# A Fourier layer with a soft mixture of experts on one core: expert weight loads moved away from the last batch's two DRAM round trips, and each round trip's loads put on two DMA queues

## The chip, the core and the metric

The kernel runs on one core of a Trainium2 chip. The engines named here are PE (TensorE, matrix products), DVE (VectorE), ACT (ScalarE), POOL (GpSimd) and SP (SyncE, which in this kernel only issues DMAs). The metric is device time in microseconds (us) of one execution, the median of several. Before the change it is 558.88 us (three runs, 558.2 to 559.1).

## The reference: what is computed

For each of 8 batches x is 2496 tokens by 256 channels, float32. A real Fourier transform runs along the tokens, then a complex linear layer over the channels, a soft threshold at 0.01 and the inverse transform. The result, 19968 tokens by 256, goes through a soft mixture of 8 experts with 4 slots each:

```
logits = x @ phi                                    # 19968 x 32
d = softmax of logits over the tokens (each slot over all 19968)
slot_input = d.T @ x                                # 32 x 256
h = max(slot_input[e] @ w1[e], 0); slot_out[e] = h @ w2[e]      # w1: 8 x 256 x 1024, w2: 8 x 1024 x 256
c = softmax of logits over the slots (each token over its 32)
out = c @ slot_out
```

The softmax over tokens joins all batches: the expert layers can start only when the last batch has been through the whole chain, and the output only when the expert layers are done.

## The kernel before, in words

The transform of length 2496 is split into 39 by 64. A main loop of 40 steps (8 batches with 5 groups of frequencies each) does the forward transform, the complex layer and the threshold. PE, DVE, ACT and POOL all work in it. Times in the code's tables count a step as 4 units, and TB is the time at which the last step's work is over.

Behind the loop each batch has a chain (c_stages, and last_chain for batch 7) that forms logits, their exponentials and the weighted sums of the slots without ever forming the inverse transform of all channels. In it the data changes its layout twice, and each time through DRAM: `g_sb` is written to `gd` and read back as `gp` with the axes exchanged (first trip), and `ea` is written to `ed` and read back as `eb` (second trip). The reads are in pieces of 32 numbers, 128 bytes. For batches 0 to 6 the chain runs inside the main loop; for batch 7 nothing is left to run beside it except the transposes `pt` of batches 6 and 7 (tp_t: PE transposes, ACT and DVE copy the result to the tiles `T`) and the sums `pr` of batch 6.

The chain of batch 7 on the engines is: `pg` (PE), `g_sb` (ACT), write `gd`, read `gp`, `pL` (PE), maximum and `L`, `pm`, `pb`, exponential `ee` (ACT), `pe` (PE), `ea`, write `ed`, read `eb`, `pd` (PE), `dd` (DVE), `pr`, `psl`. Then come the expert layers: first `hps` (all 16 tiles of w1), `hs`, `pht`, then `po` (all 16 tiles of w2); and then the output: `cin` (stored combine weights of batches 0 to 5, read back), `chl` (their split in two parts by ACT and DVE), `pc`, `so`, `prep`, and 78 products `pq` whose copies `ost` are written out.

The expert weights are 32 loads of 512 KB (16 MB), w1 first; load number i is called wi here, from w0 to w31. The table `PLAN["T_"]["wl"]` gives for each load its time against TB and the tile it goes to: 'r', 'a', 'x', 'T', 'h', 't' name pools of tiles that are free by then ('x' and 'T' are two half loads of 256 KB each). The pool behind 'h' (hl_tile, tag "hl") has 9 buffers (NHL, the third number of `PLAN["nw"]`), which the output tiles `ost` use later. A tile pool gives its buffers out in turn, and a load into a buffer that was used waits for the last reader of what was in it.

Every engine works in the order in which its instructions were recorded, so an instruction that waits holds up everything behind it on its engine. All DMAs are issued by SP on one queue. Each DMA takes the next of 8 semaphores in turn (DMAHW0 to DMAHW7), and waits at issue until the DMA eight places before it has landed.

## Time and profile before

| | before |
|---|---|
| time, median of 3 runs | 558.88 us (558.2 to 559.1) |
| time of the profiled execution | 556.67 us |
| its span, first to last instruction | 554.5 us |
| granted TensorE clock | 0.994 |
| PE busy | 520.4 us (94%) |
| DVE, ACT, POOL busy | 433.3, 299.7, 287.2 us |
| DMA traffic | 115.95 MB, mean 209 GB/s |
| chain that ended last | PE 64%, DVE 16%, DMA 9%, ACT 4%, issue 4% |

The profiled execution is 2.2 us faster than the median of the runs; its span is 2.17 us shorter than its own time. In a row of a timeline stand start and duration in us from the span's start, engine, line, operation, what is written and read, and in brackets how long the engine was idle before and what ended that. "SPq" rows are DMA issues on SP's queue; their duration is the issue, not the transfer. A row of the chain of waits has start, duration and what the program's end hung on then. A row of the windows has the stretch, its length, busy us and instruction counts of PE, PE's weight load, DVE, ACT and POOL, the granted clock, the mean busy share of the 16 DMA engines, and GB/s. Line 227 is the helper that issues a DMA from SP, line 174 the one that records the operations of DVE, ACT and POOL, line 233 the one for matrix products.

### The profile page before, as it was taken

What the parts mean: (1) busy time and instruction counts of PE and PEld (TensorE: products, weight loads), DVE (VectorE), ACT (ScalarE), POOL (GpSimd) and SP (SyncE); (2) the same over time, 40 slices, a digit from 0 to 9 for tenths busy, and PEclk for the clock granted to TensorE, in tenths of its full rate; (3) what the DMA queues carried; (4) which work ended last, traced back from release to release, by engine and by line L of the source; (5) the groups of instructions that cost most, each with busy time, mean ns of one, the idle gap of its engine ahead of it and who ended that gap; (6) DMA issues with size and microseconds to landing.
All of it is one profiled execution on the core that took longest, in us unless ns stands there. A gap on an engine that the chain in (4) does not pass through costs nothing.

```text
span 554.5 us, 11971 instructions
## 1 busy us (share of the span) xinstructions
PE 520.4 (94%) x4455; PEld 448.9 (81%) x4455; DVE 433.3 (78%) x853; ACT 299.7 (54%) x662; POOL 287.2 (52%) x262
## 2 busy tenths in 40 slices
...
GB/s 304 187 172 168 133 201 168 193 175 201 192 179 180 178 189 189 164 190 201 177 178 180 186 202 155 241 211 204 186 83 130 105 177 299 379 252 363 365 373 356
DMA packets 90181, 115.95 MB, mean 209 GB/s; under 512 B 46482, under 2 KB 65872, under 8 KB 90124
## 3 DMA queue, kind: packets, MB, share of 16 engines
...
q14 instruction: 22, 0.18, 0.1%
...
## 4 chain that ended last, share of the span: by engine, by line
PE 64%; DVE 16%; DMA 9%; ACT 4%; issue 4%; SPq 1%; POOL 1%; ACTq 0%; DVEq 0%; POOLq 0%
PE py L233 14%; PE px L233 9%; PE pq L233 8%; PE pa L233 7%; PE pk L233 6%; PE pt L595 4%; PE pr L233 3%; DMA eb<-ed 3%; PE pc L1083 2%; DVE mx L174 2%; DVE xtl L174 2%; DMA ed<-ea 2%; DVE ut L174 1%; DVE clpL L174 1%; PE pe L233 1%
## 5 line engine op out<-in xcount | busy, mean ns | idle before, releaser
L174 POOL TENSOR_TENSOR rt<-ut,rt 128x512 f32<-128x512 f32 x79 | 112.4, 1423 | 21.1 <-DVE rt L174 17.4
L174 POOL TENSOR_TENSOR xsl<-xsm,xsh 128x256 fp32r<-128x256 f32 x78 | 59.8, 766 | 108.1 <-DVE xsh L174 76.0
L174 POOL TENSOR_TENSOR xl<-xr,xh 117x512 fp32r<-117x512 f32 x74 | 100.9, 1364 | 16.4 <-ACT xh L174 8.6
L233 PE MATMUL px<-smov,ap 128*128 128x128 f32 x640 | 86.1, 278 | 2.5 <-DVE xsm L174 1.6
L233 PEld LDWEIGHTS px<-smov,ap 128*128 128x128 f32 x640 | 80.5, 193 | 8.7 <-PE pa L233 2.5
L174 ACT CAST xth<-px 128x512 fp32r<-128x512 f32 x80 | 46.9, 586 | 64.1 <-PE py L233 34.2
L174 DVE SCALAR_TENSOR_TENSOR ut<-py,pk,k 128x256 f32<-128x256 f32 x160 | 69.4, 474 | 12.9 <-PE py L233 11.0
L174 ACT COPY ast<-pa 128x512 f32<-128x512 f32 x77 | 45.3, 588 | 57.7 <-PE pa L233 57.6
L174 DVE TENSOR_TENSOR xtl<-px,xth 128x512 fp32r<-128x512 f32 x80 | 54.5, 682 | 20.8 <-ACT xsm L174 20.6
L233 PE MATMUL py<-xth,nwsh 128*128 128x256 f32 x160 | 53.4, 334 | 0.0
L174 DVE TENSOR_SCALAR rt<-ut 128x512 f32<-128x512 f32 x69 | 50.9, 738 | 0.5
L233 PE MATMUL pk<-xsh,w_rh 128*128 128x256 f32 x160 | 48.2, 301 | 0.0
L174 ACT COPY T<-pt 128x512 f32<-128x512 f32 x70 | 42.0, 601 | 9.0 <-PE pt L595 7.3
L595 PE MATMUL pt<-pk,rt 128*128 128x128 f32 x320 | 45.8, 273 | 0.9 <-DVE dd L174 0.6
L233 PE MATMUL pk<-xsl,w_rh 128*128 128x256 f32 x160 | 45.4, 284 | 0.3 <-POOL xsl L174 0.3
L233 PE MATMUL pk<-xsh,w_rl 128*128 128x256 f32 x160 | 45.1, 282 | 0.0
L233 PE MATMUL py<-xtl,wdh 128*128 128x256 f32 x160 | 44.7, 279 | 0.0
L233 PE MATMUL py<-xtl,nwsh 128*128 128x256 f32 x160 | 44.7, 279 | 0.0
L233 PE MATMUL py<-xth,wdl 128*128 128x256 f32 x160 | 44.7, 279 | 0.0
L233 PE MATMUL py<-xth,wdh 128*128 128x256 f32 x160 | 44.6, 279 | 0.0
L233 PE MATMUL py<-xth,nwsl 128*128 128x256 f32 x160 | 44.6, 279 | 0.0
L233 PE MATMUL pq<-rhs,ct 128*128 128x512 f32 x156 | 41.8, 406 | 0.3 <-DVE ost L174 0.3
...
## 6 DMA issues: line engine op xcount, KB each, us to landing
...
```

What stands on the lines that cost most here:

```text
L174: return lambda *a, **k: self.tc.keep_in_program_order(f(*a, **k))
L233: tc.keep_in_program_order(nc.tensor.matmul(**kw))
L595: tc.keep_in_program_order(nc.tensor.transpose(out=out, in_=in_, identity=identity))
L1083: nc.tensor.transpose(out=pc[:, i * P1 : (i + 1) * P1], in_=chls[b][x][:, 2 * (r + i) : 2 * (r + i) + 2].rearrange("p g h s -> p (g h s)") ...
```

## The change

Three things change.

Place and time of the weight loads. Four loads (w3 to w6) move to 42 units before TB, in the main loop, into the room of two tiles (`atr`) that only the head of the program needs; these tiles move from the main loop's pool to one of their own ("hd"). No load stands any more between the end of the main loop and the first trip, nor behind the read of the first trip. Four loads (w15 to w18, 'H') are issued by ACT, behind the copies of `L`. The last 13 stand behind the read of the second trip on SP: w19 and w20 as 'T', w21 and w22 as 'x', w23 to w28 as 'h', w29 to w31 as 't'.

Queues. `gp` is read by four DMAs, two on SP and two on ACT, and `eb` by two, one on SP and one on ACT. Both reads are recorded earlier in the program's order (the numbers behind TB).

Transposes. The first group of batch 7's transposes (pt_0) is recorded at TB + 0.9 and so stands ahead of `pL` rather than behind `pr` of batch 6.

```
--- before.py
+++ after.py
@@ -142,7 +142,7 @@
     "ko": 0.915,
     "to": 0.7,
     "late": {'6': {'cms': [19.75, 19.71, 860.75, 862, 864, 865], 'pd': [20.36, 20.37], 'pr': [31.55, 31.6, 31.65, 31.7, 31.75], 'pL': [5.4, 5.8], 'pm': 6.875, 'pb': 7.325, 'pe': [8.75, 9.75], 'pg': [0.875, 1.275], 'fr': {'sinv': 0, 'm2': 0, 'f1': 0, 'suni': 0}}, '5': {'pg': [1.1, 1.8], 'pL': [4.95, 5.75], 'pm': 6.8, 'pb': 7.15, 'pe': [9.2, 9.9], 'pd': [13.8, 14.8], 'pr': [15.0, 17.25, 19.5, 21.75, 24.0]}, '4': {'pr': [18.4, 20.49, 24.49, 28.49, 32.49]}},
-    "T_": {'wl': [[-45, 'r'], [-44, 'r'], [-43, 'r'], [-31.0, 't'], [-30.7, 't'], [-29.4, 't'], [-27.6, 't'], [-27.8, 't'], [-11, 'a'], [-10.3, 'a'], [-9.6, 'a'], [-7.5, 'x'], [-6.4, 'x'], [1.11, 'x'], [1.07, 'h'], [1.08, 'h'], [1.09, 'h'], [1.1, 'h'], [1.11, 'h'], [13.55, 'h'], [13.1, 'h'], [13.6, 'h'], [13.6, 'h'], [13.61, 't'], [13.61, 't'], [13.61, 't'], [13.61, 't'], [13.61, 't'], [13.7, 'T'], [13.7, 'T'], [13.7, 'T'], [13.7, 'T']], 'cl': 16, 'cp': 46.5, 'ct': 46.6, 'du': [[-4.5, 0], [-2.4, 0], [1.2, 0]], 'd1': [5, 2, 4, 0, 0, 0], 'cm': [19.9, 19.91, 19.92, 25, 25.1, 25.2], 'cm7': [18, 20, 22, 23, 25, 27], 'ye': 0.2, 'te': [[5.6, 0.2], [5.5, 0.4]], 'pg': [-7, -3.25, -0.35], 'yt': 0.5, 'wr': -30.6, 'tp': [0, 0.9, 1.05, 0.5], 'tt': [[-0.4, 0.5, 0.6, 0.7, 0.8], [12, 12.1, 12.2, 12.3, 12.4]], 'z': 13.55, 'th': [0.1, 0.12], 'tl': [0.2, 0.25]},
+    "T_": {'wl': [[-45, 'r'], [-44, 'r'], [-43, 'r'], [-42, 'e'], [-41.9, 'e'], [-41.8, 'e'], [-41.7, 'e'], [-31.0, 't'], [-30.7, 't'], [-29.4, 't'], [-27.8, 't'], [-27.6, 't'], [-11, 'a'], [-10.3, 'a'], [-9.6, 'a'], [10.3, 'H'], [10.31, 'H'], [10.32, 'H'], [10.33, 'H'], [13.56, 'T'], [13.57, 'T'], [13.58, 'x'], [13.59, 'x'], [13.6, 'h'], [13.6, 'h'], [13.6, 'h'], [13.6, 'h'], [13.6, 'h'], [13.6, 'h'], [13.61, 't'], [13.61, 't'], [13.61, 't']], 'cl': 16, 'cp': 46.5, 'ct': 46.6, 'du': [[-4.5, 0], [-2.4, 0], [1.2, 0]], 'd1': [5, 2, 4, 0, 0, 0], 'cm': [19.9, 19.91, 19.92, 25, 25.1, 25.2], 'cm7': [18, 20, 22, 23, 25, 27], 'ye': 0.2, 'te': [[5.6, 0.2], [5.5, 0.4]], 'pg': [-7, -3.25, -0.35], 'yt': 0.5, 'wr': -30.6, 'tp': [0, 0.9, 1.05, 0.5], 'tt': [[-0.4, 0.5, 0.6, 0.7, 0.8], [0.9, 12, 12.1, 12.2, 12.3]], 'z': 13.55, 'th': [0.1, 0.12], 'tl': [0.2, 0.25]},
     "f1": [1.5, 2.15],
     "ap1": 1.9,
     "f0": 0.2,
@@ -182,6 +182,7 @@
     pp = ctx.enter_context(tc.tile_pool(name="pp", bufs=2, space=bass.MemoryType.PSUM))
     dr = ctx.enter_context(tc.tile_pool(name="dr", bufs=2, space=bass.MemoryType.DRAM))
     wcp = ctx.enter_context(tc.tile_pool(name="wc", bufs=1, side="right"))
+    hdp = ctx.enter_context(tc.tile_pool(name="hd", bufs=1, side="left"))
     wm = tc.tile_pool(name="wm", bufs=1, side="left")
     wa = tc.tile_pool(name="wa", bufs=1, side="right")
     wmp, wap = wm.__enter__(), wa.__enter__()
@@ -349,6 +350,9 @@
 
     qps, at0, atr = {}, [], []
 
+    def hd_tile(h, name):
+        return hdp.tile([128, 2 * (K1 - KG) * NP], F32, tag=f"hd{h}", name=name)
+
     def q_mm(i, h):
         qd, k = divmod(i, 2)
         if k == 0:
@@ -409,7 +413,7 @@
         yield t_[0]
         for h in range(2):
             at0.append(wtile([128, G, S], F32, ("L", "ee")[h], f"at0_{h}").rearrange("p g s -> p (g s)")[:, : 2 * KG * NP])
-            atr.append(wmp.tile([128, 2 * (K1 - KG) * NP], F32, tag=f"at{h}", name=f"atr{h}"))
+            atr.append(hd_tile(h, f"atr{h}"))
         for i in range(6):
             for h in range(2):
                 q_mm(i, h)
@@ -842,7 +846,7 @@
     w1 = [(0, c, 2 * j + q) for q in range(2) for c in range(2) for j in range(4)]
     w2 = [(1, h, 2 * j + q) for h in range(2) for q in range(2) for j in range(4)]
     wlist = w1 + w2
-    wbuf = {}
+    wbuf, early = {}, []
 
     def at(t, fn, *a):
         def one():
@@ -870,7 +874,16 @@
             src = t["moe_w1"][e, h * 128 : h * 128 + 128, :]
         else:
             src = t["moe_w2"][e, h * 512 : h * 512 + 512, :].rearrange("(p f) d -> p (f d)", f=4)
-        if loc == "r":
+        q = aq if loc.isupper() and loc != "T" else sp
+        loc = loc if loc == "T" else loc.lower()
+        if loc == "e":
+            k = len(early) % 2
+            if k == 0:
+                early.append(hd_tile(len(early) // 2, f"we{i}"))
+            else:
+                early.append(early[-1])
+            parts = [early[-1][:, k * F : k * F + F]]
+        elif loc == "r":
             parts = [wtile([128, F], F32, "wr", f"w{i}")]
         elif loc == "a":
             parts = [wtile([128, F], F32, "ap", f"w{i}")]
@@ -880,10 +893,10 @@
             parts = [hl_tile(f"w{i}")]
         else:
             tags = {"x": ("xth", "xtl"), "T": ("T", "T")}[loc]
-            parts = [wtile([128, F // 2], F32, tags[q], f"w{i}_{q}") for q in range(2)]
+            parts = [wtile([128, F // 2], F32, tags[z], f"w{i}_{z}") for z in range(2)]
         n = F // len(parts)
-        for q, r in enumerate(parts):
-            sp(out=r, in_=src[:, q * n : q * n + n])
+        for z, r in enumerate(parts):
+            q(out=r, in_=src[:, z * n : z * n + n])
         wbuf[(w, h, e)] = parts
 
     def hl_tile(name):
@@ -952,20 +965,13 @@
             mm(out=ps[:, :n], lhsT=sinv, rhs=psb[b][:, ks, :], start=True, stop=True)
             A.copy(out=g_sb[:, ks, :].rearrange("p k s -> p (k s)"), in_=ps[:, :n])
             sp(out=gd.rearrange("n (c k) s -> (n c) k s", c=2)[:, ks, :], in_=g_sb[:, ks, :])
-        yield TB + 1
+        yield TB + 0.68
         gp = wtile([Q1, G, S], F32, "gp", f"gp{b}")
-        for r in range(R):
-            ge = 22 if r < 2 else 20
-            p0 = r * 2 * K1
-            sp(
-                out=gp[p0 : p0 + 2 * K1, :ge, :],
-                in_=gd[22 * r : 22 * r + ge].rearrange("g k s -> k g s"),
-            )
-            if ge < G:
-                sp(
-                    out=gp[p0 : p0 + 2 * K1, ge:, :],
-                    in_=gd[22 * r : 22 * r + G - ge].rearrange("g k s -> k g s"),
-                )
+        for r, g0, g1, q in ((0, 0, 22, sp), (1, 0, 22, aq), (2, 20, 22, aq), (2, 0, 20, sp)):
+            q(
+                out=gp[r * 2 * K1 : (r + 1) * 2 * K1, g0:g1, :],
+                in_=gd[22 * r : 22 * r + g1 - g0].rearrange("g k s -> k g s"),
+            )
         L = wtile([P1, G, S], F32, "L", f"L{b}")
         mx = wtile([P1, 4, S], F32, "mx", f"mx{b}")
         yield TB + 7
@@ -1015,10 +1021,10 @@
         ed = dr.tile([2 * K1, NP, S], F32, tag="ed", name=f"ed{b}")
         sp(out=ed.rearrange("k (r g) s -> (k r) g s", r=R), in_=ea)
         pools["L"] = L
-        yield TB + 13.5
+        yield TB + 12.07
         eb = wtile([128, K1, S], F32, "gp", f"eb{b}")
         for c in range(2):
-            sp(out=eb[c * 64 : c * 64 + 64], in_=ed[c * K1 : c * K1 + K1, :N2].rearrange("k n s -> n k s"))
+            (sp, aq)[c](out=eb[c * 64 : c * 64 + 64], in_=ed[c * K1 : c * K1 + K1, :N2].rearrange("k n s -> n k s"))
         dd = wtile([128, K1, S], F32, "dd", f"dd{b}")
         yield TB + 12.5
         dummy(T_["d1"][5])
```

How the instructions stand. SP, around the first trip, before (w_0 and w_1 are half loads of expert weights; names as above):

```order
L227 DMA w_0_6522<-in_moe_w 128x512 [waits DVE_49,PE_49]
L227 DMA w_1_6523<-in_moe_w 128x512 [waits PE_49]
L227 DMA gd_6529<-g_sb_6528 128x384 [waits DMAHW0_49,Activation_49]
L227 DMA w_0_6536<-in_moe_w 128x512 [waits DMAHW1_49,DVE_49,PE_49]
L227 DMA w_1_6537<-in_moe_w 128x512 [waits PE_49]
L227 DMA gd_6529<-g_sb_6528 128x128 [waits DMAHW3_49,Activation_49]
L227 DMA gd_6529<-g_sb_6528 128x128 [waits DMAHW4_49,Activation_49]
L227 DMA gp_6637<-gd_6529 40x22x32 [waits DMAHW4_49,DMAHW5_49,DMAHW3_49,DMAHW0_49]
L227 DMA gp_6637<-gd_6529 40x22x32 [waits DMAHW6_49]
L227 DMA gp_6637<-gd_6529 40x20x32 [waits DMAHW7_49]
L227 DMA gp_6637<-gd_6529 40x2x32
L227 DMA w_6644<-in_moe_w 128x1024 [waits DVE_49,DMAHW1_49,PE_49,Pool_49]
```

and with the change, from the last write of `gd` on (two more writes of `gd` stand ahead of it, with no weight load between):

```order
L228 DMA gd_6534<-g_sb_6533 128x128 [waits DMAHW4_49,Activation_49]
L228 DMA gp_6606<-gd_6534 40x22x32 [waits DMAHW4_49,DMAHW5_49,DMAHW3_49,DMAHW2_49]
L228 DMA gp_6606<-gd_6534 40x20x32 [waits DMAHW7_49]
L228 DMA ed_6714<-ea_6701 120x704 [waits DMAHW5_49,DVE_49,Activation_49]
L228 DMA eb_6748<-ed_6714 64x20x32 [waits DMAHW5_49,DMAHW1_49,DMAHW6_49,DMAHW0_49,PE_49]
L228 DMA w_0_6812<-in_moe_w 128x512 [waits DMAHW0_49,PE_49,Pool_49]
L228 DMA w_1_6813<-in_moe_w 128x512 [waits DMAHW1_49,PE_49,Pool_49]
```

The two weight loads (four halves) that stood between the writes of `gd`, the seven issues behind `gp` and the one between `ed` and `eb` are gone from SP; the first weight loads behind `eb` go to tiles of tag "T", and wait for PE and POOL, which used these tiles last.

ACT, from the issue of the reads of `gp` to the four weight loads, with the change (before, there is no DMA on ACT, and pt_0's copy stands behind the copies of `ea`):

```order
L231 DMA gp_6606<-gd_6534 40x22x32
L231 DMA gp_6606<-gd_6534 40x2x32
L174 COPY T_3_5759<-pt_3_0_6618 128x512
L174 COPY zrow_6635<-dd_6479 1x128
L174 COPY T_4_5760<-pt_4_0_6630 128x512
L174 COPY T_0_0_6650<-pt_0_0_6644 128x512
L174 COPY L_6611<-pL_0_6660 117x352
L174 COPY L_6611<-pL_1_6664 117x352
L231 DMA w_6692<-in_moe_w 128x1024
L231 DMA w_6694<-in_moe_w 128x1024
L231 DMA w_6696<-in_moe_w 128x1024
L231 DMA w_6698<-in_moe_w 128x1024
```

and on to the read of `eb`:

```order
L174 ACTIVATE ee_6700<-ee_6700 117x352 x2
L174 COPY ea_6701<-pe_0_6707 120x352
L174 ACTIVATE fo<-fo 128x1
L174 COPY T_1_0_6746<-pt_1_0_6741 128x512
L231 DMA eb_6748<-ed_6714 64x20x32
L174 COPY T_2_0_6764<-pt_2_0_6757 128x512
L174 COPY T_3_0_6778<-pt_3_0_6771 128x512
```

ACT now issues two reads of `gp` between copies of batch 6's transposes, four weight loads ahead of the exponential `ee`, and half of `eb` behind the copy of pt_1.

SP, the end of the weight loads, with the change:

```order
L228 DMA w_1_6825<-in_moe_w 128x512 [waits DMAHW7_49]
L228 DMA w_6828<-in_moe_w 128x1024 [waits DMAHW0_49]
L228 DMA w_6830<-in_moe_w 128x1024 [waits DMAHW1_49]
L228 DMA w_6832<-in_moe_w 128x1024 [waits DMAHW2_49]
L228 DMA w_6834<-in_moe_w 128x1024 [waits DMAHW3_49]
L228 DMA w_6836<-in_moe_w 128x1024 [waits DMAHW4_49]
L228 DMA w_6838<-in_moe_w 128x1024 [waits DMAHW5_49,PE_49]
L228 DMA w_6840<-in_moe_w 128x1024 [waits DMAHW6_49]
L228 DMA w_6842<-in_moe_w 128x1024 [waits DMAHW7_49]
L228 DMA w_6844<-in_moe_w 128x1024 [waits DMAHW0_49]
L228 DMA cin_6846<-c_dr_128 117x512 [waits DMAHW1_49]
L228 DMA cin_6846<-c_dr_128 117x192 [waits DMAHW2_49]
```

The wait on PE stands at the tenth load into tiles of tag "hl" (w28; four were issued by ACT, and five stand in the rows ahead of it). It takes the buffer of w15, which the last products of the first expert layer read. Before, nine loads went there, and no weight load behind `eb` waited for the expert layer.

More of the change, by code (lines that the diff above doesn't have):

```diff
@@ L184, in fourier_soft_moe_kernel @@
     wcp = ctx.enter_context(tc.tile_pool(name="wc", bufs=1, side="right"))
+    hdp = ctx.enter_context(tc.tile_pool(name="hd", bufs=1, side="left"))
     wm = tc.tile_pool(name="wm", bufs=1, side="left")
@@ L350, in fourier_soft_moe_kernel, with hd_tile @@
     qps, at0, atr = {}, [], []
+    def hd_tile(h, name):
+        return hdp.tile([128, 2 * (K1 - KG) * NP], F32, tag=f"hd{h}", name=name)
     def q_mm(i, h):
@@ L411, in head @@
             at0.append(wtile([128, G, S], F32, ("L", "ee")[h], f"at0_{h}").rearrange("p g s -> p (g s)")[:, : 2 * KG * NP])
-            atr.append(wmp.tile([128, 2 * (K1 - KG) * NP], F32, tag=f"at{h}", name=f"atr{h}"))
+            atr.append(hd_tile(h, f"atr{h}"))
         for i in range(6):
@@ L844, in fourier_soft_moe_kernel @@
     wlist = w1 + w2
-    wbuf = {}
+    wbuf, early = {}, []
     def at(t, fn, *a):
@@ L872, in load_w @@
             src = t["moe_w2"][e, h * 512 : h * 512 + 512, :].rearrange("(p f) d -> p (f d)", f=4)
-        if loc == "r":
+        q = aq if loc.isupper() and loc != "T" else sp
+        loc = loc if loc == "T" else loc.lower()
+        if loc == "e":
+            k = len(early) % 2
+            if k == 0:
+                early.append(hd_tile(len(early) // 2, f"we{i}"))
+            else:
+                early.append(early[-1])
+            parts = [early[-1][:, k * F : k * F + F]]
+        elif loc == "r":
             parts = [wtile([128, F], F32, "wr", f"w{i}")]
@@ L882, in load_w @@
             tags = {"x": ("xth", "xtl"), "T": ("T", "T")}[loc]
-            parts = [wtile([128, F // 2], F32, tags[q], f"w{i}_{q}") for q in range(2)]
+            parts = [wtile([128, F // 2], F32, tags[z], f"w{i}_{z}") for z in range(2)]
         n = F // len(parts)
-        for q, r in enumerate(parts):
-            sp(out=r, in_=src[:, q * n : q * n + n])
+        for z, r in enumerate(parts):
+            q(out=r, in_=src[:, z * n : z * n + n])
         wbuf[(w, h, e)] = parts
```

25 lines of the change are left out of this document (9 added, 16 removed).

## The prediction

> **What bounds the kernel now.** I read the chain of waits first, from the end of the main loop on, because the change touches only what lies behind it. Start, duration, and what the end hung on:
>
> ```profile
> 449.45 3.40 DMA gd<-g_sb
> ...
> 453.96 3.44 DMA gp<-gd
> ...
> 457.54 1.41 PE pL L233 x4
> ...
> 468.57 4.24 DMA eb<-ed
> ...
> 478.46 5.36 PE hps L233 x48
> ```
>
> Three waits on DRAM stand on the path: 3.40 us for the write of `gd`, 3.44 for the last piece of `gp`, 4.24 for the second half of `eb`. Nothing else runs long enough to cover them. Next SP's timeline, for what stood in the queue around them, and for two earlier trips with little beside them (344 and 420 us):
>
> ```profile
> 420.80 0.33 SPq L227 DMA_DIRECT2D gd<-g_sb  x1
> 422.97 2.73 SPq L227 DMA_DIRECT2D gp<-gd  x4
> ...
> 447.39 0.87 SPq L227 DMA_DIRECT2D w<-in_moe_w  x2
> 448.79 0.99 SPq L227 DMA_DIRECT2D gd<-g_sb  x2
> 452.99 2.65 SPq L227 DMA_DIRECT2D gp<-gd  x4
> 455.81 3.25 SPq L227 DMA_DIRECT2D w<-in_moe_w  x7
> 464.96 0.36 SPq L227 DMA_DIRECT2D ed<-ea  x1
> 465.36 1.22 SPq L227 DMA_DIRECT2D w<-in_moe_w  x1
> 467.95 2.29 SPq L227 DMA_DIRECT2D eb<-ed  x2
> 470.28 15.00 SPq L227 DMA_DIRECT2D w<-in_moe_w  x16
> 485.57 7.54 SPq L227 DMA_DIRECT2D cin<-c_dr  x12
> ```
>
> ```profile
> 344.62 0.35 SPq L227 DMA_DIRECT2D ed<-ea  x1
> 347.43 1.40 SPq L227 DMA_DIRECT2D eb<-ed  x2
> ```
>
> What the DMA engines moved in those stretches (the last two columns are their busy share and GB/s):
>
> ```profile
> 449.50:451.50 2.00, 2.00 (x16) 1.74 (x15) 1.71 (x3) 1.05 (x3) 0.00 (x0) 1.00 0.85 301
> 454.00:456.50 2.50, 0.94 (x9) 0.70 (x7) 1.38 (x2) 1.03 (x3) 0.00 (x0) 1.00 0.81 126
> 468.50:469.50 1.00, 1.00 (x11) 1.00 (x10) 0.82 (x2) 0.71 (x2) 1.00 (x3) 1.00 0.87 357
> 470.00:472.50 2.50, 1.45 (x14) 1.21 (x12) 1.81 (x3) 1.17 (x2) 1.46 (x4) 1.00 1.05 153
> ```
>
> 301 GB/s at 450 us cannot be 128 KB of `gd`: the weight loads issued just ahead go through first. 357 GB/s at 469 is the load of 465.36, ahead of `eb`. At 454 to 456.5 and 470 to 472.5 the 128-byte pieces run alone, at 126 and 153 GB/s: there no weight load is in the way, though the loads were issued at 455.81. So weight loads hold the write of the first trip and the read of the second; the read of the first they do not touch.
>
> **First trip: 1.7 us off.** The last write of `gd` is issued at 449.45 as now, with the queue empty. A `gd` of 320 KB on an idle queue took 422.97 - 420.80 = 2.17 us; this one has 64 KB, so 2.17 is the upper end. I take 2.0: `gp` can be issued at 451.6 instead of 452.99. From there to `pL` it took 457.54 - 452.99 = 4.55, which gives 456.15 with nothing gained by two queues. Two queues save at least nothing; at most the half of the 2.65 us of issues, 1.3. Since 330 KB at 126 GB/s take 2.6 us by themselves, I take 0.3: 455.85. A floor stands just there, pt_0, which is now ahead of `pL` on PE:
>
> ```profile
> 452.54 2.40 PE L595 MATMUL pt<-pk,rt 128*128 128x128 f32 x20 [0.59 <-DVE dd L174]
> ```
>
> PE is through with these at 454.94, and eight more at the 2.40/20 = 0.12 us of this row end at 455.9. Whatever two queues save beyond 0.3 us disappears behind pt_0. `pL` starts at 455.85: 1.7 us earlier (0.7 if `gp` also waits for ACT, below; 1.7 is the top).
>
> ACT's two reads stand behind a copy that ended at 452.04, and are late by 0.4 us against SP's; the transfers of SP's two cover that. The four weight loads on ACT fall into this idle time:
>
> ```profile
> 451.45 0.59 ACT L174 COPY T<-pt 128x512 f32<-128x512 f32 x1 [0.29 <-PE pt L595]
> 459.01 0.99 ACT L174 COPY L<-pL 117x352 f32<-117x352 f32 x2 [3.89 <-DVE mx L174]
> 462.33 0.93 ACT L174 ACTIVATE ee<-ee 117x352 f32<-117x352 f32 x2 [2.33 <-DVE ee L174]
> 467.55 0.58 ACT L174 COPY T<-pt 128x512 f32<-128x512 f32 x1 [3.23 <-PE pt L595]
> ```
>
> No DMA was issued by ACT before. By SP's rows an issue is 0.35 to 0.6 us, four are 1.4 to 2.4, and ACT was idle 2.33 ahead of `ee`: cost 0, at most 0.1. Their 2.1 MB at some 400 GB/s are through about when `ed` is written, so I leave that write at its 467.95 - 464.96 = 2.99 (2.81 for the one at 344.62, with nothing behind it).
>
> **Second trip: 1.4 us off.** Before, 472.81 - 467.95 = 4.86 us from the first issue to landing (468.57 + 4.24). Now: 0.75 to the first byte (for the `gd` of 420.80 nothing moved before 421.5, row below), 320 KB at 153 GB/s = 2.1, and 0.4 to the semaphore (the row above ends at 472.5, `eb` landed at 472.81); 0.2 more because ACT's half stands behind the copy of pt_1, which for pt_0 in the ACT row above ended at 468.13, 0.2 behind 467.95. Together 3.45, so 1.4 off. If the halves ran truly side by side, 2.4; if the four half loads issued behind `eb` (1 MB, 2.6 us at 400 GB/s) mix into it, up to 4.9.
>
> ```profile
> 420.50:421.50 1.00, 1.00 (x14) 0.69 (x7) 0.44 (x3) 0.28 (x1) 1.00 (x2) 1.00 0.00 0
> ```
>
> [...]
>
> `pd`, and with it `hps`, thus comes 1.7 + 1.4 = 3.1 us earlier: 475.4 instead of 478.46. All w1 are there by then.
>
> **The new wait takes 1.9 us of it back.** w28 is the tenth load into nine buffers, and SP waits at it until the first expert layer has read w15, its last tile. Behind it stand w29 to w31 and `cin`. What the layer's end released, and who needs `cin`:
>
> ```profile
> 486.42 0.69 DVE L174 COPY hs<-hps 128x512 f32<-128x512 f32 x1 [1.52 <-PE hps L233]
> 492.68 0.96 DVE L174 TENSOR_TENSOR chl<-cin,chl 117x512 fp32r<-117x512 f32 x2 [0.23 <-ACT chl L174]
> 494.57 0.42 DVE L174 TENSOR_TENSOR so<-po,so 128x256 fp32r<-128x256 f32 x1 [0.94 <-ACT so L174]
> ```
>
> ```profile
> 490.84 0.87 ACT L174 CAST chl<-cin 117x512 fp32r<-117x512 f32 x2 [2.78 <-DMA cin<-c_dr]
> 492.03 0.87 ACT L174 CAST chl<-cin 117x512 fp32r<-117x512 f32 x2 [0.32 <-DMA cin<-c_dr]
> ```
>
> The layer ends at 486.42 - S, with S = 3.1 the gain so far. From w28's issue: 0.75 to the first byte, four loads of 524 KB at 407 GB/s = 5.15, `cin` of batch 0 (322 KB) 0.9, landing 0.45: 7.25 us. So ACT gets `cin` at 493.67 - S, 2.83 - S later than the 490.84 of before. In-order DVE ends `chl` of batch 1 as much later than 493.64, and only then can do `so`, which before had 494.57 - 493.64 = 0.93 us to spare. `so` moves earlier by S - 2.83 + 0.93 = S - 1.9. For S = 3.1 that is **1.2 us**. (`po` itself waits for w28 to w31 only some 0.4 us, so `cin` decides.) Were S only 1.9, nothing would be gained.
>
> **Output phase.** It begins with `so` and is a fixed amount of work:
>
> ```profile
> 501.00:519.00 18.00, 14.99 (x78) 11.26 (x76) 14.79 (x27) 12.47 (x26) 2.74 (x2) 1.00 1.00 400
> 519.00:521.00 2.00, 2.00 (x14) 1.68 (x15) 1.75 (x4) 1.11 (x3) 0.00 (x0) 1.00 0.33 131
> ```
>
> DMA is full, but it runs dry at 519, waiting for the engines. So the engines, which start with `so`, set the pace to there, and all of it moves by the same 1.2 us.
>
> **Main loop: 0, with an end at 3 us.** Four loads, 2.1 MB, go to about 356 to 361 us:
>
> ```profile
> 354.00:358.00 4.00, 4.00 (x45) 3.58 (x38) 3.90 (x11) 1.92 (x6) 1.02 (x2) 1.00 0.91 237
> 358.00:364.00 6.00, 6.00 (x52) 5.31 (x51) 5.38 (x11) 2.88 (x6) 5.34 (x5) 1.00 1.02 407
> 364.50:369.50 5.00, 5.00 (x55) 4.19 (x53) 4.54 (x8) 3.29 (x8) 3.68 (x5) 1.00 0.06 20
> ```
>
> ```profile
> 369.18 0.33 SPq L227 DMA_DIRECT2D gd<-g_sb  x1
> ```
>
> ```profile
> 376.66 0.87 ACT L174 CAST chpL<-gp 120x352 fp32r<-120x352 f32 x2 [2.11 <-DMA gp<-gd]
> ```
>
> The backlog ended at about 364.3 (the last of these rows has a share of 0.06), and 2.1 MB at 407 GB/s are 5.2 us: 369.5. Batch 5's `gd`, issued at 369.18, moves its first byte at about 370. The hole of 5 us at share 0.06 is the cover, and it is just filled. If it were not enough, each us would count, since ACT already waits 2.11 us for this very `gp`.
>
> **The sum.** The profiled execution took 556.67 us (span 554.5 and 2.17 around it), 2.2 us less than the median of the runs. 1.7 + 1.4 - 1.9 - 0 = 1.2 us off: 555.5 for such an execution, and 558.88 - 1.2 = 557.7 as a median.
>
> **Rivals.**
> 1. *Two queues move small pieces faster.* For it: the third and fourth issue of `gp` were slow, as if the queue made the pace; against it: a DMA share of 0.81 to 1.05 while they ran. `eb` would land in 2.4 us, S = 4.1, gain 2.2: 556.7. Two pages disagree here: the Trainium skill's "Perfetto Trace Analysis", section "DMA Optimizations", says that balancing DMAs over issuing engines may help where descriptor generation is the limit; its "DMA: Bandwidth & Descriptors", section "Rules for kernel authors", says that two halves by partitions serialize and that a second issuing engine only saves issue time. The busy share goes with the second; chance 0.12.
> 2. *The half loads behind `eb` take the place of the load ahead of it.* They wait for pt_2 to pt_4, which end about when `eb` is issued, so they are in flight with it. Against it: SP's half of `eb` is ahead of them in its queue. `eb` keeps its 4.86, S = 1.7, and the change loses 0.2: 559.1. Chance 0.2.
> 3. *Slower: the early loads push batch 5's first trip.* At the 237 GB/s of 354 to 358, 2.1 MB take 8.9 us, the backlog lasts to 373.2, `gd` is 3.2 us late, PE idles as long: 557.7 + 3.2 = 560.9. It gives a slower kernel from a backlog to 372.3 on. Against it: 407 GB/s right behind that stretch. Chance 0.13.
> 4. *`cin` doesn't decide* (SP gets to w28 later than I think, or the split is quicker): what is left is S less the 0.4 of `po`, 2.7: 556.2. Chance 0.05.
>
> **How the numbers follow.** The forecast has 0.5; its own range is 557.0 to 558.6, from S between 2.2 and 3.8. 0.2% of this kernel, about what a measurement can tell from no change, is 1.1 us, so the forecast lies on that edge: I give 0.28 of its 0.5 to faster, 0.22 to the same. Faster: 0.28 + 0.12 + 0.05 = 0.45, and 0.01 for rival 2's better end, 0.46. Same: 0.22 + 0.14 of rival 2 = 0.36. Slower: 0.13 + 0.05 of rival 2 = 0.18. The range that leaves out 2 in 10 runs from 556.5 (below rivals 1 and 4 by little) to 559.7 (beyond rival 2, in rival 3).
>
> **What would show it.** `pL` at 455.8 right behind pt_0, with `gp` landing at about the same time; `eb` landing 3.4 us behind its issue; `hps` 3.1 us earlier; then an idle DMA stretch of about 3 us ahead of w28, and ACT's first `chl` at about 490.6, hardly earlier than before, though `po` ends at 491.5. At 376 us ACT's wait for `gp` stays near 2.1. Wrong would be: no idle stretch ahead of w28; `chl` earlier by as much as `hps`; `eb` taking 2.5 or 4.9 us; a longer wait at 376.

## The result: 1.3% slower, and the profile after

The changed kernel takes 564.8 us in the median (six executions, 562.3 to 569.3). Its ratio to the kernel before, measured side by side, is 1.013 with a 95% interval from 1.010 to 1.017. One of the six executions of the kernel before took 1011.6 us and is left out of the ratio as slow; the other five took 555.9 to 559.1. I had forecast 557.7 us. The profiled execution took 568.35 us (span 566.2), one of the two longest of the six; the one before took 556.67 (span 554.5). So this profile shows 11.7 us of loss, twice that of the medians; what is known of the difference between executions stands in the last section.

Both spans can be cut at the same eight events. Each leg is read from the rows of the two timelines: the end of the last copy into `g_sb`; the start of `pL`; the issues of `ed` and of the first half of `eb`; the starts of `pd` and `hps`; DVE's `so`; the end.

| leg, us | before | after | difference |
|---|---|---|---|
| main loop, to the end of `g_sb` | 449.43 | 451.78 | +2.35 |
| `g_sb` to `pL` (first trip) | 8.11 | 6.22 | -1.89 |
| `pL` to the issue of `ed` | 7.42 | 7.35 | -0.07 |
| `ed` issued to `eb` issued | 2.99 | 4.32 | +1.33 |
| `eb` issued to `pd` | 4.99 | 5.18 | +0.19 |
| `pd` to `hps` | 5.52 | 8.39 | +2.87 |
| `hps` to `so` | 16.11 | 21.10 | +4.99 |
| `so` to the end | 59.93 | 61.86 | +1.93 |
| sum | 554.50 | 566.20 | +11.70 |

One leg became shorter, the first trip. The chain of waits of the kernel after (start, duration, what the end hung on) shows where the others grew:

```profile
353.28 10.40 DMA w<-in_moe_w
363.70 8.36 DMA ap<-adr
372.19 2.05 PE px L234 x8
...
458.16 1.19 PE pL L234 x4
...
469.80 5.00 DMA eb<-ed
474.85 2.50 PE pd L234 x4
...
483.24 5.36 PE hps L234 x48
...
493.96 8.77 DMA cin<-c_dr
```

SP's and ACT's rows give the fourth leg:

```profile
465.35 0.33 SPq L228 DMA_DIRECT2D ed<-ea  x1
...
469.67 0.68 ACTq L231 DMA_DIRECT2D eb<-ed  x1
```

In the chain, weight loads and then `ap`, an input of the main loop that is read back from DRAM, stand on the path from 353 to 372 us. The chain of before had no DMA there until batch 5's trip:

```profile
369.18 2.17 DMA gd<-g_sb
372.67 3.89 DMA gp<-gd
```

SP's timeline after (start, duration of the issue, operation) gives the reason; `we` are the early loads:

```profile
355.59 1.81 SPq L228 DMA_DIRECT2D we<-in_moe_w  x2
359.43 0.34 SPq L228 DMA_DIRECT2D c_dr<-cb  x1
359.81 1.13 SPq L228 DMA_DIRECT2D we<-in_moe_w  x2
362.52 1.76 SPq L228 DMA_DIRECT2D ap<-adr  x2
```

`ap` is issued behind all four early loads, 3.0 us later than before, and its bytes stand behind theirs:

```profile
359.55 1.25 SPq L227 DMA_DIRECT2D ap<-adr  x2
```

That row is from before. TensorE's timeline after has both of its long waits on DMA (in brackets: idle time ahead, and what ended it):

```profile
372.19 2.05 PE L234 MATMUL px<-smov,ap 128*128 128x128 f32 x8 [3.08 <-DMA ap<-adr]
...
474.85 2.50 PE L234 MATMUL pd<-eb,pk 128*128 128x320 f32 x4 [2.71 <-DMA eb<-ed]
```

The windows after (stretch, length, busy us of PE, weight load, DVE, ACT, POOL, granted clock, DMA share, GB/s) show the other two losses:

```profile
471.00:474.00 3.00, 1.09 (x8) 0.86 (x8) 0.69 (x1) 1.06 (x2) 0.00 (x0) 1.00 1.14 171
474.50:481.00 6.50, 6.15 (x38) 2.93 (x42) 1.33 (x4) 0.30 (x1) 0.00 (x0) 0.50 1.05 394
485.60:492.30 6.70, 6.70 (x67) 2.49 (x60) 0.98 (x3) 0.87 (x3) 0.00 (x0) 1.00 0.04 17
492.30:498.00 5.70, 5.28 (x88) 2.96 (x86) 0.29 (x2) 0.28 (x2) 0.00 (x0) 1.00 0.97 367
```

After the wait of 2.71 us for `eb` the granted clock is 0.50 for 6.5 us, and `pd` to `hps` takes 8.39 us instead of 5.52. And the DMA engines stand idle (share 0.04) from 485.6 to 492.3, while SP waits at w28; the four loads and `cin` that should have run there come afterwards.

### The profile page after: what moved, and what is told of

Same layout as the page of the kernel before. It is cut to its first block, busy times and chain, and to the rows that moved or that the text cites. A ratio compares the mean times of both kernels' runs of the same rounds, so it can differ in the third digit from the quotient of the medians.

```text
span 566.2 us, 11953 instructions
## 1 busy us (share of the span) xinstructions
PE 528.2 (93%) x4455; PEld 452.8 (80%) x4455; DVE 432.6 (76%) x853; ACT 299.6 (53%) x662; POOL 286.8 (51%) x262
## 3 DMA queue, kind: packets, MB, share of 16 engines
q1 hardware_dynamic: 86840, 112.82, 61.1%
## 4 chain that ended last, share of the span: by engine, by line
PE 63%; DVE 15%; DMA 12%; ACT 4%; issue 3%; SPq 1%; POOL 0%; ACTq 0%; DVEq 0%; POOLq 0%
PE py L234 13%; PE px L234 9%; PE pq L234 8%; PE pa L234 7%; PE pk L234 6%; PE pt L599 5%; PE pr L234 3%; DMA eb<-ed 3%; PE q L234 2%; DMA w<-in_moe_w 2%; PE pc L1089 2%; DMA gp<-gd 2%; DMA cin<-c_dr 2%; DVE xtl L174 1%; DMA ap<-adr 1%
```

## The experiments

Four theories, one for each leg that grew. A: the early loads stand ahead of `ap`. B: SP's wait at w28 empties the DMA engines. C: a TensorE that waits too long for `eb` is given half its clock. D: the loads that ACT sends hold the write of `ed`. A fifth, E: the half loads behind SP's half of `eb` hold ACT's half. The ratios are to the kernel before on the same chip, with 95% intervals; the legs are those of the one profiled execution, cut as above, which lies up to 3.6 us off the median of its kernel. The leg from `pL` to the issue of `ed`, 7.35 to 7.45 us, and 9.09 in b1_queues_only, is left out.

| kernel | median, us | ratio | `g_sb` end | first trip | `ed` | `eb` to `pd` | `pd` to `hps` | `hps` to `so` | `so` to end |
|---|---|---|---|---|---|---|---|---|---|
| before | 558.0 to 558.5 | 1 | 449.43 | 8.11 | 2.99 | 4.99 | 5.52 | 16.11 | 59.93 |
| after | 564.8 | 1.013 [1.010, 1.017] | 451.78 | 6.22 | 4.32 | 5.18 | 8.39 | 21.10 | 61.86 |
| e1_early_spread | 567.3 | 1.017 [1.013, 1.021] | 450.19 | 7.95 | 5.17 | 5.15 | 7.85 | 21.82 | 60.13 |
| e2_no_ring_wait | 562.3 | 1.009 [1.006, 1.012] | 454.67 | 6.22 | 3.07 | 4.92 | 5.54 | 16.65 | 61.78 |
| e3_dummies | 565.3 | 1.014 [1.010, 1.018] | 454.31 | 6.22 | 4.25 | 6.75 | 5.44 | 18.94 | 60.04 |
| c1_three_undone | 561.3 | 1.005 [1.002, 1.008] | 450.62 | 7.76 | 4.15 | 6.77 | 5.44 | 16.12 | 61.09 |
| e5_loads_behind_gp | 565.4 | 1.015 [1.011, 1.020] | 449.84 | 6.97 | 2.85 | 5.27 | 6.98 | 21.07 | 60.00 |
| c2_trips_clear | 558.2 | 1.000 [0.998, 1.002] | 449.07 | 6.41 | 2.89 | 5.01 | 7.02 | 16.12 | 61.46 |
| c3_eb_one_queue | 557.0 | 0.997 [0.994, 0.999] | 448.70 | 7.20 | 2.89 | 4.43 | 5.51 | 16.28 | 60.67 |
| c4_one_queue | 556.7 | 0.998 [0.995, 1.000] | 449.45 | 6.25 | 3.15 | 4.51 | 5.51 | 16.12 | 61.89 |
| c5_early_back | 558.6 | 1.000 [0.997, 1.003] | 451.18 | 6.22 | 3.13 | 4.77 | 7.11 | 16.17 | 60.42 |
| c6_ring_wait_back | 561.8 | 1.006 [1.004, 1.008] | 449.51 | 6.30 | 3.06 | 4.84 | 7.03 | 21.49 | 60.25 |
| b1_queues_only | 579.8 | 1.039 [1.037, 1.040] | 449.86 | 15.09 | 3.14 | 16.31 | 8.32 | 16.11 | 60.18 |
| c7_six_dummies | 557.0 | 0.998 [0.996, 1.000] | 450.97 | 6.26 | 2.97 | 4.52 | 5.52 | 16.12 | 61.12 |

**Early loads elsewhere.** In the table of the plan (times in units ahead of or behind TB):

```diff
-[-42, 'e'], [-41.9, 'e'], [-41.8, 'e'], [-41.7, 'e'], ...
+..., [-20.6, 'e'], [-20.3, 'e'], ..., [-7.8, 'e'], [-7.5, 'e'], ...
```

> The change, but the four early loads go to places where the DMA engines were idle in the main loop: two at about 406 us, two at about 434 us, instead of 355.6 to 361 us. Theory A (the early loads cost the main loop 2.4 us because they stand ahead of the loads of ap): TensorE's idle 3.08 us ahead of px at 372 us shrinks to under 0.5, the last copy into g_sb ends again near 449.4 instead of 451.8, and the time falls by 2.4 us, or by 3.4 with the clock that the idle time cost: 561.4 to 562.4 for a median of 564.8. Rival (the early loads are harmless; the main loop lost its 2.4 us by the throttle alone): g_sb still ends at 451 or later and the time stays within 1 us of 564.8.

The main loop did what theory A says: no wait for `ap`, and `g_sb` ends at 450.19. The median was 567.3 all the same, no better than after (the intervals overlap), since I had put the second pair badly. SP was held by the trip of batch 6, and the pair went out just ahead of the writes of `gd`:

```profile
446.33 1.22 SPq L228 DMA_DIRECT2D we<-in_moe_w  x2
447.64 2.89 SPq L228 DMA_DIRECT2D gd<-g_sb  x3
```

```profile
449.00:452.00 3.00, 3.00 (x26) 2.79 (x26) 2.93 (x5) 1.61 (x4) 0.00 (x0) 1.00 0.92 356
```

356 GB/s in the window of the small write: the first trip took 7.95 us instead of 6.22, as it had before the change. By accident this undoes the first trip alone, and shows its gain to come from the loads taken away ahead of `gd`. One more row of this run, from ACT's timeline:

```profile
471.48 1.07 ACT L174 COPY T<-pt 128x512 f32<-128x512 f32 x2 [2.71 <-DMA ed<-ea]
```

ACT's half of `eb` waits in ACT's own queue until `ed` has landed, and the copies of TensorE's transposes wait behind it: here a DMA on ACT's queue made ACT wait 2.71 us.

**No wait at w28.**

```diff
-[13.6, 'h'], [13.6, 'h'], [13.6, 'h'], [13.6, 'h'], [13.6, 'h'], [13.6, 'h'], [13.61, 't'], ...
+[13.6, 'h'], [13.6, 'h'], [13.6, 'h'], [13.6, 'h'], [13.6, 'h'], [13.61, 't'], [13.61, 't'], ...
```

> The change, but w28 goes into a buffer that is free by then, so that the tenth load into nine buffers, and SP's wait for the end of the first expert layer, are gone. Theory B (that wait leaves the DMA engines idle for 6.7 us and makes w28 to w31 and cin late): no idle DMA stretch between 480 and 492 us, ACT's first chl at about 492 instead of 501.5, and so follows the experts: hps + 16.1 as before, some 4.5 to 5 us earlier than with the wait in an execution like the profiled one; the median at 560 to 561. Rival (po is late by the halved clock and waits for nothing else; cin has slack): the idle stretch goes, but so moves by less than 1 us and the median stays at 564 to 565.

Windows of this run:

```profile
476.00:482.00 6.00, 5.02 (x54) 2.74 (x58) 2.43 (x8) 0.48 (x2) 0.00 (x0) 1.00 1.06 394
485.00:492.00 7.00, 7.00 (x76) 2.99 (x72) 1.27 (x5) 1.16 (x5) 0.00 (x0) 1.00 1.03 409
```

The idle stretch is gone (share 1.03), `hps` to `so` is 16.65 us instead of 21.10, and the median fell by 2.5 us, though the intervals of the two ratios overlap. Theory B holds in the leg (4.5 us) and in part in the median, where I had expected 4 or 5. In the first window the clock stayed at 1.00, although TensorE had waited 2.36 us for `eb`.

**Dummies ahead of `pd`.**

```diff
-'d1': [5, 2, 4, 0, 0, 0]
+'d1': [5, 2, 4, 0, 0, 20]
```

> The change, and 20 matmuls of 128x128 more (2.5 us, results unused) on TensorE while it waits for eb. Theory C (the 2.71 us without a matmul ahead of pd make the throttle grant 0.50 for the next 7 us): the granted clock stays at 1.00 from 474 to 482, pd to hps takes 5.5 us instead of 8.4, hps and all behind it, SP's wait at w28 too, come 2.9 us earlier where the drop had happened; the runs lie closer together and the median at 562 to 563. Rival (the drop belongs to the load on the chip, not to the idle time): 0.50 is granted there all the same, and the time stays at 564 to 566.

TensorE's timeline, and a window behind it:

```profile
474.41 4.63 PE L234 MATMUL dps<-pk 128*128 128x128 f32 x40
478.88 1.24 PE L234 MATMUL pd<-eb,pk 128*128 128x320 f32 x4
```

```profile
478.50:484.50 6.00, 5.25 (x59) 3.02 (x62) 2.42 (x8) 0.48 (x2) 0.00 (x0) 1.00 1.03 395
```

The clock stayed at 1.00 and `pd` to `hps` took 5.44 us: theory C holds there. But each dummy is two matmuls on the engine, so the twenty took 4.6 us instead of my 2.5, and pushed `pd` back by 1.6 us (6.75 instead of 5.18 from `eb`'s issue). What the clock gave, the dummies took, and the median stayed (565.3, where I had expected 562 to 563).

**The three together** (the three diffs above):

> The three edits of the runs before together: early loads in idle places, w28 in a free buffer, 20 dummy matmuls. By the three theories hps comes at about 478 us (483.2 - 2.4 - 2.9), so at 494.1, and the time is that of the kernel before within 1 us: 557.5 to 559.5, since the first trip's 1.7 us are eaten by ed (1.5 us longer). If something else costs time, the median stays above 560.5; if the trips give what was forecast of them, it falls to 556 or less.

561.3: above the 560.5 at which something else had to be missing. The legs name it: the first trip lost as in e1_early_spread (7.76), `ed` 4.15, and 1.6 us of dummies. `hps` to `so` is back at 16.12.

**ACT's loads back on SP, behind `gp`.**

```diff
-[10.3, 'H'], [10.31, 'H'], [10.32, 'H'], [10.33, 'H'], ...
+[1.05, 'h'], [1.06, 'h'], [1.07, 'h'], [1.08, 'h'], ...
```

> The change, but the four loads that ACT sends ahead of ee go on SP's queue right behind its half of gp (some 5.5 us earlier). Theory D (those loads, in flight until 467.6, hold the write of ed, which took 4.45 us instead of the 2.99 that I left it at): they are through by about 462, ed takes 2.8 to 3.0 us, so eb and all behind it come 1.4 us earlier and the median falls by 1.4 us, to about 563.4. Rival (ed is long for another reason, such as its landing behind other writes): it stays at 4.4 us and the time at 564.8.

```profile
464.23 0.36 SPq L228 DMA_DIRECT2D ed<-ea  x1
...
467.08 0.67 ACTq L231 DMA_DIRECT2D eb<-ed  x1
```

`ed` took 2.85 us instead of 4.32, as theory D says. The loads ahead of `ee` are not the whole of it, though: with them at the same place `ed` took 3.07 in e2_no_ring_wait, and 4.15 to 5.17 in four others. After the loads, the DMA engines of the kernel after stay at a share of 0.05, less than one engine of the 16, from 467.95 to 469.15 us, and `ed` counts as landed only behind that; in e2_no_ring_wait they fall silent at 470.84 and `ed` has landed by 471.31. What keeps that engine busy is not shown. The median did not fall (565.4, from 562.5 to 568.9 in four executions): 1.4 us do not show in it.

**All out of the way.** Early loads behind the `ap` of 398 us and at 429 us, six loads behind `gp` on SP, w28 in a free buffer, both trips still on two queues:

```diff
-[-42, 'e'], [-41.9, 'e'], [-41.8, 'e'], [-41.7, 'e'], ..., [10.3, 'H'], [10.31, 'H'], [10.32, 'H'], [10.33, 'H'], ...
+..., [-24, 'e'], [-24, 'e'], ..., [-10.25, 'e'], [-10.2, 'e'], ..., [1.05, 'h'], ..., [1.1, 'h'], ...
-[13.6, 'h'] x6, [13.61, 't'] x3
+[13.6, 'h'] x3, [13.61, 't'] x4
```

> The change with its three losses moved out of the way: two early loads behind the ap of 398 us and two at about 429 us, none ahead of gd; six loads behind gp on SP, none from ACT; w28 in a free buffer; no dummies. Both trips still go on two queues. Expected: g_sb ends at 449.4 as in the kernel before, pL at 455.8 (first trip 1.7 us off), ed 3.0 us, but eb still 5.0 us, since the half loads behind SP's half mix with ACT's half: hps at about 476.9 and a median of 556.5 to 557.5. If TensorE's wait for eb again exceeds 2.6 us, the clock halves and it is 2.9 us more: 559.5 to 560.5.

Main loop, first trip, `ed` and `eb` as expected to 0.4 us; the time, 558.2 us, is that of the kernel before and lies between the two ranges that I had given. The clock fell behind a wait of 2.29 us for `eb` (`pd` to `hps` 7.02), and `so` to the end took 1.5 us longer.

**`eb` on one queue.**

```diff
-            (sp, aq)[c](out=eb[c * 64 : c * 64 + 64], ...
+            sp(out=eb[c * 64 : c * 64 + 64], ...
```

> The run c2_trips_clear, but both halves of eb on SP's queue, so that every half load stands behind both of them, and ACT's copies no longer queue behind a DMA that waits for ed. Theory E (the half loads on the other queue are what held eb; two queues cost there and give nothing): eb takes 3.3 to 3.6 us, pd comes 1.4 us earlier than in c2_trips_clear, hps at about 475.4, and the median is 555 to 556. Rival (two queues do split the read, the issue of the second half counts): eb takes as long or longer than in c2_trips_clear, and the median stays or rises.

Before this edit (first row) and with it:

```profile
470.80 1.45 PE L234 MATMUL pd<-eb,pk 128*128 128x320 f32 x4 [2.29 <-DMA eb<-ed]
```

```profile
470.64 1.32 PE L234 MATMUL pd<-eb,pk 128*128 128x320 f32 x4 [1.70 <-DMA eb<-ed]
```

`eb` to `pd` takes 4.43 us instead of 5.01: theory E has the sign and 0.6 of its 1.4 us. The profiles of the changed kernel without the 20 dummies agree: 4.92 to 5.27 us with `eb` on two queues (five), 4.43 to 4.84 on one (five). The clock stays up, and `hps` comes 1.7 us earlier, most of it by the clock (`pd` to `hps` 5.51 instead of 7.02). The median of 557.0 misses the 555 to 556 expected. This kernel is faster than the one before: 0.997, interval 0.994 to 0.999.

**`gp` on one queue too.**

```diff
-((0, 0, 22, sp), (1, 0, 22, aq), (2, 20, 22, aq), (2, 0, 20, sp))
+((0, 0, 22, sp), (1, 0, 22, sp), (2, 0, 20, sp), (2, 20, 22, sp))
```

> The run c3_eb_one_queue, and gp's four pieces on SP's queue too, in the order of before: no DMA on ACT at all. By my account of the first trip two queues were worth 0.3 us and pt_0 bounds the rest: pL no more than 0.3 to 0.5 us later, the median within 0.5 us of c3_eb_one_queue. Rival (two queues carry the first trip): pL 1 us or more later behind gp, the median 1 us up.

```profile
452.56 3.28 PE L599 MATMUL pt<-pk,rt 128*128 128x128 f32 x28 [0.58 <-DVE dd L174]
455.70 1.41 PE L234 MATMUL pL<-gp,pk 120*117 120x352 f32 x4
...
470.78 1.32 PE L234 MATMUL pd<-eb,pk 128*128 128x320 f32 x4 [2.04 <-DMA eb<-ed]
```

`pL` starts right behind pt_0 with `gp` from a single queue, and the first trip is 6.25 us, no longer than with two. In c3_eb_one_queue and e5_loads_behind_gp, where two queues bring `gp` and loads stand behind SP's half, it was 7.20 and 6.97, with TensorE waiting 0.83 and 0.58 us for `gp`; in c2_trips_clear, with the same two queues and loads, it was 6.41 without a wait, so the loss is not there in every execution. The median is the same as with two queues (556.7 and 557.0).

**Early loads back.** c4_one_queue with the early loads at 355.6 to 361 us again:

```diff
-[-24, 'e'], [-24, 'e'], ..., [-10.25, 'e'], [-10.2, 'e'], ...
+[-42, 'e'], [-41.9, 'e'], [-41.8, 'e'], [-41.7, 'e'], ...
```

> The run c4_one_queue with one thing put back: the four early loads at 355.6 to 361 us, as in the change. Theory A (they stand ahead of the loads of ap): TensorE idles 2 to 3 us ahead of px at 369 to 372, the last copy into g_sb ends 1 to 5 us later than 449.4 (the four kernels with the early loads there showed 449.8 to 454.7, those without 448.7 to 450.6), and the median is 2 to 4 us above the 556.7 of c4_one_queue. Rival (the main loop takes it, and what was seen there was chance): g_sb at 449 to 450 and the median within 0.7 us of c4_one_queue.

```profile
372.00 2.05 PE L234 MATMUL px<-smov,ap 128*128 128x128 f32 x8 [2.94 <-DMA ap<-adr]
```

The wait returns and `g_sb` ends 1.7 us later. In the five profiled executions with the early loads there, TensorE waits 2.15 to 3.77 us ahead of this `px` (in e3_dummies, with 2.39, the profile names DVE's `rt` as what came last); where they stand elsewhere it doesn't wait there. What the wait does to the end of `g_sb` varies: 449.84 us in e5_loads_behind_gp, 454.67 in e2_no_ring_wait. The median is 1.9 us up, against 2 to 4 expected, but the intervals of the two ratios overlap: the wait is shown, its price in the median only roughly.

**The wait at w28 back.** c4_one_queue with

```diff
-[13.6, 'h'] x3, [13.61, 't'] x4
+[13.6, 'h'] x4, [13.61, 't'] x3
```

> The run c4_one_queue with one thing put back: w28 is the tenth load into the nine buffers, so SP waits for the end of the first expert layer. Theory B: the seven loads ahead are through at 479, w28 goes out at about 484.4, w31 lands at 490.3, cin at 491.7, and so, which had followed hps by 16.1 us, follows cin by 3.7: 495.4 instead of 492.4, 3 us slower, 559.7 in the median. Rival (TensorE's own work on po covers it): so stays at 492.4 and the median within 0.7 us of c4_one_queue.

SP's row for w28 to w31 and the same window with and without the wait (the second row is c6, the third c4):

```profile
486.12 1.75 SPq L228 DMA_DIRECT2D w<-in_moe_w  x4
```

```profile
479.50:486.50 7.00, 7.00 (x72) 2.52 (x68) 0.66 (x3) 0.87 (x3) 0.00 (x0) 1.00 0.08 30
```

```profile
479.50:486.50 7.00, 7.00 (x77) 3.01 (x72) 1.27 (x5) 1.16 (x5) 0.00 (x0) 1.00 1.02 381
```

Seven us in which the DMA engines move 30 GB/s instead of 381. `hps` to `so` grows from 16.12 to 21.49 us, the median from 556.7 to 561.8, and the intervals are apart. Theory B holds, and costs 5 us, not 3. Not all of it is `cin`. TensorE waited for w28 to w31 too, and ACT's part of `so` then waited for TensorE:

```profile
493.88 0.62 PE L234 MATMUL po<-w,z 128*32 128x256 f32 x2 [1.38 <-DMA w<-in_moe_w]
495.69 3.52 PE L234 MATMUL po<-w,z 128*32 128x256 f32 x26 [1.19 <-DMA w<-in_moe_w]
```

```profile
499.25 0.37 ACT L174 CAST so<-po 128x256 fp32r<-128x256 f32 x1 [2.03 <-PE po L234]
```

Behind these two waits the granted clock was 0.50 from 495.8 to 499.2 us, and 26 products took 3.52 us; at the pace of c4_one_queue (112 in 6.25 us) they take 1.45. DVE was through with `chl` at 497.96 and did `so` at 499.65. By these rows I estimate 3.7 us for the late `cin` and 1.7 for the clock.

**Only the queues.** The kernel before, with nothing changed but the queues of `gp` and `eb`:

> The kernel before, with nothing changed but the queues: gp's and eb's pieces on SP and ACT as in the change, all loads where they were. If two queues move the small pieces faster, gp and eb land 0.5 to 1 us earlier each and the median falls by 0.5 to 2 us. If they only share the same 16 engines, and the loads behind SP's half now mix with ACT's half, gp's landing stays or comes up to 0.7 us later, eb's up to 0.6 us later, and the median is 558.4 to 559.7, the same or slower.

```profile
464.95 2.67 PE L233 MATMUL pL<-gp,pk 120*117 120x352 f32 x4 [9.58 <-DMA gp<-gd]
...
493.49 2.47 PE L233 MATMUL pd<-eb,pk 128*128 128x320 f32 x4 [12.96 <-DMA eb<-ed]
```

In the kernel before, the same two rows were:

```profile
457.54 1.41 PE L233 MATMUL pL<-gp,pk 120*117 120x352 f32 x4 [2.60 <-DMA gp<-gd]
...
472.94 1.32 PE L233 MATMUL pd<-eb,pk 128*128 128x320 f32 x4 [1.50 <-DMA eb<-ed]
```

Far outside both ranges: 579.8 us, 3.9% slower. Each trip loses, the first 7.0 us, the second 11.3. A part is that ACT, with copies ahead in its order, issued late: `gp` at 455.18 where SP's part went out at 453.70, and `eb` at 480.19 instead of 477.18, so 1.5 and 3.0 us. The counts by queue say how (q1 is SP's, q10 ACT's: packets, MB, share of 16 engines), first from 457 to 466 us, then from 480 to 494:

```profile
q1 hardware_dynamic: 711, 2.30, 68.8%
q10 hardware_dynamic: 980, 0.12, 9.1%
```

```profile
q1 hardware_dynamic: 1276, 4.38, 81.6%
q10 hardware_dynamic: 1296, 0.16, 7.9%
```

In the second stretch the queues moved about one packet for one, 1276 to 1296 (in the first 711 to 980). But a packet of a weight load has some 3,400 bytes (4.38 MB by 1276) and one of `eb` 128, so ACT's half of `eb` got its 160 KB through only as 4.4 MB of loads went by. This goes with the Trainium skill, "DMA: Bandwidth & Descriptors", section "Queues, rings and completion order", which says that each DMA engine takes turns between the queues packet by packet. The rule of the same page's section "Rules for kernel authors", that a second issuing engine saves nothing but issue time, understates what it can cost: 579.8 us instead of 558.5. On one queue, in the kernel before, loads issued behind the small read left it 4.99 us from issue to `pd`, where here it is 16.31.

**Six dummies.** c4_one_queue with

```diff
-'d1': [5, 2, 4, 0, 0, 0]
+'d1': [5, 2, 4, 0, 0, 6]
```

> The run c4_one_queue and six matmuls of 128x128 (float32, two passes each, 1.5 us by the 5 us that twenty took) on TensorE while it waits for eb. Theory C: executions in which that wait grows past some 2.2 us lose 1.5 us to the halved clock (pd to hps 7.0 us in the profiles of c2_trips_clear, c5_early_back and c6_ring_wait_back, 5.5 in c3 and c4); with the wait cut to some 0.5 us none does: pd to hps 5.4 to 5.6, the runs closer together and the median at 555.5 to 556.5, under 0.997 of the kernel before. Rival (the spread comes from elsewhere): the median stays at 556.7 and the spread as it was (554.7 to 558.5).

```profile
472.14 1.31 PE L234 MATMUL pd<-eb,pk 128*128 128x320 f32 x4 [0.54 <-DMA eb<-ed]
```

The wait is cut from 2.04 to 0.54 us and `pd` to `hps` is 5.52, but the median is 557.0 and the spread 554.7 to 559.6: no gain. So the spread has other sources as well. In c4_one_queue the three executions with a mean clock of 0.985 or 0.986 took 558.4 to 558.5 us, the seven with 0.988 to 0.994 took 554.7 to 557.2; in the profile of c7_six_dummies the clock fell at 400 and at 518 us, far from `eb`.

## Why the prediction was wrong

**What was right.** The first trip: forecast 1.7 us off with pt_0 as the floor, measured 1.89, with `pL` right behind pt_0; the 0.3 us that I gave to two queues is not needed (c4_one_queue). The pieces differ from the sum: `gp` was issued 1.66 us behind `g_sb`, where I had 2.17, and it is pt_0 that sets the time. The loads on ACT did fit into its idle time ahead of `ee` (2.34 us idle as before). The wait at w28 was where I had put it. Rival 3 had the right kind of mechanism, early loads that push a DMA of the main loop, with a chance of 0.13.

**"Main loop: 0"** failed. I asked whether the backlog would be through before batch 5's `gd`, issued at 369.18, and took that for the victim. The load that stood right behind the early loads on SP was `ap` of the next step, issued at 359.55 before, and `px` wanted it at 369.1, where TensorE's wait began. My own estimate of the backlog's end, 369.5, was late for that. Price at the end of `g_sb`: 2.35 us in the profile, 1.7 in c5_early_back, but 0.4 in e5_loads_behind_gp and 5 in e2_no_ring_wait and e3_dummies, so it is not one number.

**"I leave that write at 2.99"** failed. The 2.1 MB of ACT's loads were in flight until 467.7, and `ed`, issued at 465.35, took 4.32 us; with the loads earlier it took 2.85 to 3.15 (seven kernels). So a long `ed` goes with these loads in four profiles of five; e2_no_ring_wait has 3.07 with the loads in the same place, and what decides there stays open. I had noted that the loads end "about when `ed` is written" and gone on as though that were enough.

**"Second trip: 1.4 us off"** failed in two terms. Rival 2 came true: the half loads mixed into `eb`, worth 0.6 us (c2 against c3). And the sum itself was too low: with one queue and nothing ahead, `eb` took 4.4 to 4.8 us to `pd` (4.99 before), where 3.45 to landing was to replace 4.86. Its upper end was too low by its own figures: 2.6 us of half loads on top of 3.45 are 6.05, not 4.9. Windows of c4_one_queue, where `eb` was issued at 466.27, show its first bytes:

```profile
467.40:467.60 0.20, 0.20 (x5) 0.20 (x3) 0.20 (x1) 0.14 (x1) 0.20 (x2) 1.00 0.00 0
467.60:467.80 0.20, 0.20 (x4) 0.20 (x3) 0.12 (x1) 0.20 (x1) 0.20 (x1) 1.00 0.54 86
467.80:468.80 1.00, 0.93 (x9) 0.69 (x7) 0.72 (x2) 0.71 (x2) 0.89 (x3) 1.00 1.15 182
```

1.35 us to the first byte where I took 0.75, from the write of a `gd`, a transfer of another kind. So of the 1.4 us about 0.5 can be had.

**"The new wait takes 1.9 us of it back"**: right in place, mis-sized. The bill was made for an `hps` at 475.4, and for a `cin` 7.25 us behind w28's issue. `hps` came at 483.24, and the idle stretch became 6.7 us instead of 3. `cin` took 8.5 us from w28's issue in c6_ring_wait_back (486.12 to 494.66), and TensorE waited for w28 to w31 itself (1.37 and 1.17 us in the profile after, where I had said 0.4). In c6_ring_wait_back it is `po` and not `cin` that decides in the end, by the clock lost behind these waits. 5 us, not 1.9.

**What I had no term for** is the clock. I read a granted clock of 1.00 around both trips before, where TensorE waits 2.60 and 1.50 us, and took waits at their length. That the 2.60 had cost no clock was a near thing (last section). The wait of 2.71 us cost another 2.87 us behind it, and the one at 369 some 1 us in the same way (`px` took 2.05 us for its eight products).

**"Output phase: fixed"** failed by up to 2 us. It took 59.9 to 60.7 us in eight profiles without a fall of the clock between 510 and 545 us (before, e1, e3, e5, c3, c5, c6, b1), and 61.1 to 61.9 in five with a fall between 515 and 534 (after, e2, c2, c4, c7); c1 had 61.1 without one. No run was made to change it; the last section says what the clock goes by.

In the medians, the wait at w28 is 2.5 (e2 against after, intervals overlapping) to 5 (c6 against c4, intervals apart) of the 6 us lost, and the early loads up to 2 (c5 against c4, overlapping); the trips gain some 2 when nothing else is spoiled (c4, by its interval 0.1 to 2.6). How the rest divides stays open: a stall may move the next wait to where it loses the clock, which is not shown, and the executions of one kernel lie up to 7 us apart.
